# Three weight bits from ScalarE and the first block's low parts of g from VectorE, in a kernel of windowed attention and two MLPs

## The chip, the cores and the metric

The kernel runs on one core of one Trainium2 chip. The time is device microseconds of one execution; before the change the median of 3 runs is 924.38 us (921.47 to 929.18).

## The reference

Windowed attention (4 batches, 8 heads, 576 positions, head size 64, each position sees itself and the 63 before it) gives 2304 rows of 512 numbers. They go through two MLPs, and only the first of them and its weights are touched here:

```python
def _moe_ref(x, w_in, w_out) -> np.ndarray:          # x 2304 x 512
    h = x @ w_in                                       # 512 x 2048
    g = np.maximum(h, 0.0) + np.log1p(np.exp(-np.abs(h)))   # softplus
    return (g @ w_out).astype(np.float32)              # 2048 x 512
...
x = _moe_ref(x=x, **moe_kwargs)
return _moe2_ref(x=x, **moe2_kwargs)                 # sigmoid gate, 512 -> 1536 -> 512
```

The weights arrive as 8-byte floats, q, k and v as 4-byte ones.

## The kernel before, in words

**Products in three parts.** Every matrix product is made of rounded high parts and low parts: `mm3` (L362 to L365) runs high x high, high x low and low x high into the same PSUM bank. So each operand needs a high part (a rounding copy on ScalarE) and a low part (the value minus its high part).

**The first MLP.** Tokens go in five blocks of 512, 384, 384, 512 and 512 columns (b = 0 to 4). For each block and each of 16 slices f of 128 hidden units, `m1_proj` makes h (12 matmuls), `m1_act` (L382, ScalarE) the softplus into a tile "tb", `g_hi` (L389, ScalarE) its high part, `g_lo` (L395, GpSimd) its low part, and `m1_out` adds g x w_out into four PSUM banks (12 matmuls). Block b+1's attention runs between block b's products.

**The weights.** The 32 slices of w_in and w_out (i = 0 to 31, alternating after the first three; NSLOT is 32) are loaded once, during block 0, and then stay in SBUF. A slice is a 128x1024 tile of words, "raw", that holds low word and high word of each 8-byte float in turn. It is turned into 4-byte floats in "bits" by four steps and split by two more:

- `w_scale` (L118, ScalarE): the high word, read as a float and scaled by 2^-112, gives exponent and leading bits.
- `w_shift` (L123, VectorE): shifts these left by 3.
- `w_sign` (L127, VectorE): puts in the sign of the high word.
- `w_low` (L132, VectorE): puts in the low word's top three bits (shift right by 29, then or).
- `w_hi` (L138, ScalarE): the high part of the slice.
- `w_lo` (L143, GpSimd): its low part.

There are three raw tiles and three bits tiles; a raw tile is free after `w_low`, a bits tile after `w_lo`. The second MLP's 36 slices go through the same first four steps later.

**Attention, as far as it matters.** For a group of 64 positions TensorE makes scores into a PSUM tile "at" (two of them), VectorE's `att_max` (L272, L275) reads them, ScalarE takes the exponentials (L287), GpSimd's `att_norm` (L298) divides, TensorE turns the result round, and `att_values` (L345) writes into the next of the two "at" tiles. So `att_values` waits until `att_max` of an earlier group has read that tile. `att_hi` and `att_lo` (L353, L358) split the result.

**The order.** The program is one list of steps for all engines, and each engine runs its own in that order. For everything up to the second MLP the list comes from `lead_in`, a planner: it takes the steps with their costs and dependencies from `traits` (for example `"pool", 1.25` for g_lo) and plays them through, engine by engine, so that a change of costs or of engines moves steps of every engine. Filler matmuls on "ones" (L680) keep TensorE busy at the start.

## Time and profile before

| | us |
|---|---|
| median of 3 runs | 924.38 (921.47 to 929.18) |
| the profiled execution's own time | 923.64 |
| its span, first to last instruction | 921.9 |
| mean granted TensorE clock in the span | 0.993 of full speed |
| TensorE matmuls busy | 897.9 (97%) |
| VectorE, ScalarE, GpSimd busy | 507.7, 406.5, 358.9 |

The profile is of one execution, so its rows add up to its own time, 923.64 us, which stands 0.74 us below the median. Engines are PE (TensorE), PEld (its weight loads), DVE (VectorE), ACT (ScalarE), POOL (GpSimd) and SP (which issues DMAs). "x32 | 47.0, 1471 | 32.9 <-ACT" reads: 32 instructions, 47.0 us busy, 1471 ns mean, 32.9 us idle before them, ended mostly by ScalarE.

### The profile page before, as it was taken

What the parts mean: (1) busy time and instruction counts of PE and PEld (TensorE: products, weight loads), DVE (VectorE), ACT (ScalarE), POOL (GpSimd) and SP (SyncE); (2) the same over time, 40 slices, a digit from 0 to 9 for tenths busy, and PEclk for the clock granted to TensorE, in tenths of its full rate; (3) what the DMA queues carried; (4) which work ended last, traced back from release to release, by engine and by line L of the source; (5) the groups of instructions that cost most, each with busy time, mean ns of one, the idle gap of its engine ahead of it and who ended that gap; (6) DMA issues with size and microseconds to landing.
All of it is one profiled execution on the core that took longest, in us unless ns stands there. A gap on an engine that the chain in (4) does not pass through costs nothing.

```text
span 921.9 us, 13808 instructions
## 1 busy us (share of the span) xinstructions
PE 897.9 (97%) x5070; PEld 803.8 (87%) x5074; DVE 507.7 (55%) x843; ACT 406.5 (44%) x930; POOL 358.9 (39%) x312
## 2 busy tenths in 40 slices
PE   8998899999999999999999999999999999999998
PEld 6687678998989988888888999998999999999996
DVE  5999996335343645437801667656445446444443
ACT  6877666563855655634522333324222224222222
POOL 3576675342642544455831233325111115111111
PEclk9999999999999999999999999999999999999999
DMA  8645654566666676476403676545564445544441
GB/s 313 202 160 206 218 164 169 187 220 225 208 217 219 222 262 207 156 265 241 160 1 149 228 274 229 205 160 194 194 228 160 160 160 194 195 159 160 160 160 69
DMA packets 56643, 176.54 MB, mean 192 GB/s; under 512 B 6144, under 2 KB 21248, under 8 KB 51968
## 3 DMA queue, kind: packets, MB, share of 16 engines
q1 hardware_dynamic: 56576, 175.66, 54.7%
q8 instruction: 40, 0.66, 0.3%
q14 instruction: 27, 0.22, 0.1%
HBM read 138.67 MB, written 36.96 MB: 191 GB/s over the span
## 4 chain that ended last, share of the span: by engine, by line
PE 78%; DVE 8%; DMA 6%; ACT 5%; issue 3%; SPq 1%; POOL 0%; ACTq 0%; DVEq 0%
PE h L363 14%; PE h L364 14%; PE h L365 14%; PE acc L363 9%; PE acc L364 9%; PE acc L365 9%; DMA pd<-pd 3%; DVE bits L127 2%; DVE bits L123 2%; PE at L260 2%; PE at L365 2%; PE at L364 2%; PE at L363 2%; DVE bits L132 1%; ACT p L287 1%
## 5 line engine op out<-in xcount | busy, mean ns | idle before, releaser
L471 DVE TENSOR_TENSOR t<-h,t 128x384 f32<-128x384 f32 x216 | 116.9, 555 | 199.4 <-PE h L365 191.6
L477 POOL TENSOR_TENSOR g<-t,g 128x384 fp32r<-128x384 f32 x72 | 74.8, 1040 | 288.5 <-ACT g L476 278.3
L364 PE MATMUL h<-xc,wc 128*128 128x384 f32 x504 | 169.7, 337 | 0.0
L363 PE MATMUL h<-xc,wc 128*128 128x384 f32 x504 | 169.0, 335 | 0.5 <-DVE t L471 0.4
L365 PE MATMUL h<-xc,wc 128*128 128x384 f32 x504 | 169.3, 336 | 0.0
L395 POOL TENSOR_TENSOR g<-tb,g 128x512 fp32r<-128x512 f32 (+1 forms) x80 | 102.6, 1284 | 139.1 <-ACT g L389 104.6
L363 PE MATMUL acc<-g,w 128*128 128x512 f32 (+1 forms) x320 | 122.2, 382 | 0.0
L363 PE MATMUL h<-xt,w 128*128 128x512 f32 (+1 forms) x320 | 119.7, 374 | 0.8 <-DVE xt L358 0.6
L364 PE MATMUL acc<-g,w 128*128 128x512 f32 (+1 forms) x320 | 119.5, 373 | 0.0
L365 PE MATMUL acc<-g,w 128*128 128x512 f32 (+1 forms) x320 | 119.3, 373 | 0.0
L364 PE MATMUL h<-xt,w 128*128 128x512 f32 (+1 forms) x320 | 118.0, 369 | 0.0
L365 PE MATMUL h<-xt,w 128*128 128x512 f32 (+1 forms) x320 | 117.9, 369 | 0.0
L476 ACT CAST g<-t 128x384 fp32r<-128x384 f32 x72 | 37.0, 514 | 155.0 <-DVE t L471 138.0
L363 PEld LDWEIGHTS h<-xc,wc 128*128 128x128 f32 x504 | 94.6, 188 | 9.0 <-ACT t L483 1.0
L364 PEld LDWEIGHTS h<-xc,wc 128*128 128x128 f32 x504 | 94.5, 188 | 6.5
L365 PEld LDWEIGHTS h<-xc,wc 128*128 128x128 f32 x504 | 94.7, 188 | 0.0
L143 POOL TENSOR_TENSOR w<-bits,w 128x512 fp32r<-128x512 f32 x44 | 62.9, 1430 | 56.2 <-ACT w L138 44.7
L382 ACT ACTIVATE tb<-h 128x512 f32<-128x512 f32 (+1 forms) x80 | 44.1, 551 | 87.5 <-PE h L365 86.3
L132 DVE SCALAR_TENSOR_TENSOR bits<-raw,bits 128x512 uint32<-128x512 uint32 x68 | 69.5, 1022 | 1.8
L363 PEld LDWEIGHTS h<-xt,w 128*128 128x128 f32 x320 | 60.5, 189 | 9.3 <-DVE xt L358 1.1
L363 PEld LDWEIGHTS acc<-g,w 128*128 128x128 f32 x320 | 61.3, 191 | 8.2
L365 PEld LDWEIGHTS acc<-g,w 128*128 128x128 f32 x320 | 61.4, 192 | 7.8
(100 smaller groups left out, 1549.5 us busy)
## 6 DMA issues: line engine op xcount, KB each, us to landing
wc<-wcd SPq DMA_DIRECT2D x36, 1792.0 KB, 7.2
raw<-in_w SPq DMA_DIRECT2D x32, 512.0 KB, 3.7
qk<-in_qk SPq DMA_DIRECT2D x28, 512.0 KB, 5.0
wcd<-raw SPq DMA_DIRECT2D x24, 512.0 KB, 4.8
v<-in_vt SPq DMA_DIRECT2D x25, 256.0 KB, 4.2
raw<-in_wg SPq DMA_DIRECT2D x12, 512.0 KB, 4.4
raw<-in_wv SPq DMA_DIRECT2D x12, 512.0 KB, 4.6
wcd<-sumr SPq DMA_DIRECT2D x12, 512.0 KB, 5.2
```

The costliest lines, as they stand in the source:

```text
L123: nc.vector.tensor_scalar(out=t, in0=t, scalar1=3, scalar2=None, op0=ALU.logical_shift_left)
L127: nc.vector.scalar_tensor_tensor(out=t, in0=r[:, :, 1], scalar=0x80000000, in1=t, op0=ALU.bitwise_and, op1=ALU.bitwise_or)
L132: nc.vector.scalar_tensor_tensor(out=t, in0=r[:, :, 0], scalar=29, in1=t, op0=ALU.logical_shift_right, op1=ALU.bitwise_or)
L143: nc.gpsimd.tensor_tensor(out=w[:, 1, :], in0=t, in1=w[:, 0, :].bitcast(F32), op=ALU.subtract)
L363: nc.tensor.matmul(out=o, lhsT=lh, rhs=rh, start=first, stop=False)
L364: nc.tensor.matmul(out=o, lhsT=lh, rhs=rl, start=False, stop=False)
L365: nc.tensor.matmul(out=o, lhsT=ll, rhs=rh, start=False, stop=last)
L382: nc.scalar.activation(out=t, in_=h_t.pop((b, f)), func=AF.Softplus)
L395: nc.gpsimd.tensor_tensor(out=g[:, 1, :n], in0=t, in1=g[:, 0, :n].bitcast(F32), op=ALU.subtract)
L471: nc.vector.tensor_tensor(out=out, in0=a, in1=b, op=op)
L476: nc.scalar.copy(out=g[:, 0, :HALF], in_=t)
L477: nc.gpsimd.tensor_tensor(out=g[:, 1, :HALF], in0=t, in1=g[:, 0, :HALF].bitcast(F32), op=ALU.subtract)
```

## The change

Of the 32 slices of the first MLP every odd one (16) is "topped". ScalarE gets a new instruction for it, which reads the low words as integers, scales them by almost 2^-29 with a small offset, and writes them back as integers from 0 to 7: the three bits. VectorE's separate shift goes away for that slice; one instruction (`w_join`) shifts by 3 and puts the three bits in, and the sign follows. In block 0, `g_lo` goes from GpSimd to VectorE. The planner's costs follow. The second MLP's slices and blocks 1 to 4 keep the old steps.

```diff
+    def topped(i):
+        return i < NSLOT and i % 2
+
     def w_shift(i):
-        t = bits_t[i]
-        nc.vector.tensor_scalar(out=t, in0=t, scalar1=3, scalar2=None, op0=ALU.logical_shift_left)
+        t, r = bits_t[i], raw_t[i][:, :, 0]
+        if topped(i):
+            nc.scalar.activation(out=r, in_=r, func=AF.Copy, scale=2.0 ** -29 * (1 - 2.0 ** -7), bias=-0.4395)
+        else:
+            nc.vector.tensor_scalar(out=t, in0=t, scalar1=3, scalar2=None, op0=ALU.logical_shift_left)
+
+    def w_join(i):
+        t, r = bits_t[i], raw_t[i]
+        nc.vector.scalar_tensor_tensor(out=t, in0=t, scalar=3, in1=r[:, :, 0], op0=ALU.logical_shift_left,
+                                       op1=ALU.bitwise_or)
 
     def w_sign(i):
+        if topped(i):
+            w_join(i)
+        else:
+            put_sign(i)
+
+    def put_sign(i):
         t, r = bits_t[i], raw_t[i]
         nc.vector.scalar_tensor_tensor(out=t, in0=r[:, :, 1], scalar=0x80000000, in1=t, op0=ALU.bitwise_and,
                                        op1=ALU.bitwise_or)
 
     def w_low(i):
+        if topped(i):
+            put_sign(i)
+            del raw_t[i]
+            return
...
     def g_lo(b, f):
...
-        nc.gpsimd.tensor_tensor(out=g[:, 1, :n], in0=t, in1=g[:, 0, :n].bitcast(F32), op=ALU.subtract)
+        engine = nc.gpsimd if b else nc.vector
+        engine.tensor_tensor(out=g[:, 1, :n], in0=t, in1=g[:, 0, :n].bitcast(F32), op=ALU.subtract)
...
         if fn is w_shift:
-            return "dve", 0.5, 0, [(w_scale, a)], []
+            return "act" if topped(a) else "dve", 0.67 if topped(a) else 0.5, 0, [(w_scale, a)], []
...
         if fn is g_lo:
-            return "pool", 1.25, 0, [(g_hi, a, f)], []
+            return "pool" if a else "dve", 1.25 if a else 0.7, 0, [(g_hi, a, f)], []
```

In the changed file the lines are others: the shift is L132, the sign L147, the old last step L156, the join L136, ScalarE's new step L130, g_lo L420, w_hi L162, w_lo L167, the softplus L406, g_hi L413, `att_max` L296 and L299.

VectorE's order at slices 10, 11 and 12 (bits_751, bits_798, bits_808), before:

```order
L123 TENSOR_SCALAR bits_751<-bits_751 128x512
L127 SCALAR_TENSOR_TENSOR bits_751<-raw_689,bits_751 128x512
L132 SCALAR_TENSOR_TENSOR bits_751<-raw_689,bits_751 128x512
L272 SCALAR_TENSOR_TENSOR p_792<-at_771,mask_70 128x512
L275 TENSOR_REDUCE st_793<-p_792 128x4
L123 TENSOR_SCALAR bits_798<-bits_798 128x512
L127 SCALAR_TENSOR_TENSOR bits_798<-raw_705,bits_798 128x512
L132 SCALAR_TENSOR_TENSOR bits_798<-raw_705,bits_798 128x512
L123 TENSOR_SCALAR bits_808<-bits_808 128x512
L127 SCALAR_TENSOR_TENSOR bits_808<-raw_756,bits_808 128x512
L132 SCALAR_TENSOR_TENSOR bits_808<-raw_756,bits_808 128x512
```

The same slices now (bits_763, bits_805, bits_829):

```order
L132 TENSOR_SCALAR bits_763<-bits_763 128x512
L147 SCALAR_TENSOR_TENSOR bits_763<-raw_687,bits_763 128x512
L156 SCALAR_TENSOR_TENSOR bits_763<-raw_687,bits_763 128x512
L420 TENSOR_TENSOR g_771<-tb_769,g_771 128x512
L296 SCALAR_TENSOR_TENSOR p_801<-at_736,mask_70 128x512
L299 TENSOR_REDUCE st_802<-p_801 128x4
L136 SCALAR_TENSOR_TENSOR bits_805<-bits_805,raw_767 128x512
L147 SCALAR_TENSOR_TENSOR bits_805<-raw_767,bits_805 128x512
L132 TENSOR_SCALAR bits_829<-bits_829 128x512
L147 SCALAR_TENSOR_TENSOR bits_829<-raw_790,bits_829 128x512
L156 SCALAR_TENSOR_TENSOR bits_829<-raw_790,bits_829 128x512
L420 TENSOR_TENSOR g_832<-tb_826,g_832 128x512
```

Slice 11 has two instructions in place of three, and after each pair of slices stands one g_lo, which waits for ScalarE's g_hi and has the next slices behind it.

ScalarE's order at the same place, before (w9 to w11 are the high parts of slices 9 to 11):

```order
L118 ACTIVATE bits_751<-raw_689 128x512
L382 ACTIVATE tb_754<-h0_707 128x512
L138 CAST w9_759<-bits_726 128x512
L389 CAST g_763<-tb_754 128x512
L335 COPY pt_776<-at_765 128x512
L118 ACTIVATE bits_798<-raw_705 128x512
L138 CAST w10_801<-bits_751 128x512
L118 ACTIVATE bits_808<-raw_756 128x512
L382 ACTIVATE tb_816<-h1_779 128x512
L389 CAST g_831<-tb_816 128x512
L138 CAST w11_836<-bits_798 128x512
```

And now:

```order
L118 ACTIVATE bits_763<-raw_687 128x512
L406 ACTIVATE tb_769<-h0_701 128x512
L413 CAST g_771<-tb_769 128x512
L162 CAST w9_774<-bits_724 128x512
L359 COPY pt_792<-at_730 128x512
L162 CAST w10_799<-bits_763 128x512
L118 ACTIVATE bits_805<-raw_767 128x512
L130 ACTIVATE raw_767<-raw_767 128x512
L406 ACTIVATE tb_826<-h1_776 128x512
L118 ACTIVATE bits_829<-raw_790 128x512
L413 CAST g_832<-tb_826 128x512
```

The new instruction (L130) stands right behind slice 11's scaling. Slice 10's high part now stands ahead of slice 11's scaling, and g_hi ahead of slice 9's high part.

GpSimd's order there, before:

```order
L143 TENSOR_TENSOR w9_759<-bits_726,w9_759 128x512
L395 TENSOR_TENSOR g_763<-tb_754,g_763 128x512
L143 TENSOR_TENSOR w10_801<-bits_751,w10_801 128x512
L395 TENSOR_TENSOR g_831<-tb_816,g_831 128x512
L143 TENSOR_TENSOR w11_836<-bits_798,w11_836 128x512
L143 TENSOR_TENSOR w12_861<-bits_808,w12_861 128x512
```

And now:

```order
L167 TENSOR_TENSOR w9_774<-bits_724,w9_774 128x512
L167 TENSOR_TENSOR w10_799<-bits_763,w10_799 128x512
L167 TENSOR_TENSOR w11_853<-bits_805,w11_853 128x512
L167 TENSOR_TENSOR w12_863<-bits_829,w12_863 128x512
L167 TENSOR_TENSOR w13_903<-bits_834,w13_903 128x512
```

The low parts of g are gone from between the weights' low parts; only attention's divisions remain there.

## Rows read from the trace of the kernel before

**Rows 1.** The page: each engine's busy time, share of the span, instructions.

```profile
PE 897.9 (97%) x5070; PEld 803.8 (87%) x5074; DVE 507.7 (55%) x843; ACT 406.5 (44%) x930; POOL 358.9 (39%) x312
```

**Rows 2.** Windows: length; PE, PEld, DVE, ACT, POOL busy; clock; DMA share; GB/s.

```profile
25.00:145.00 120.00, 109.47 (x656) 87.79 (x657) 112.11 (x141) 85.90 (x184) 81.30 (x57) 0.97 0.58 192
...
105.00:110.00 5.00, 2.79 (x20) 2.39 (x21) 4.93 (x7) 4.16 (x7) 3.78 (x3) 0.70 0.91 289
...
140.00:145.00 5.00, 4.92 (x19) 4.09 (x20) 4.90 (x9) 3.54 (x6) 3.01 (x3) 0.66 0.33 113
```

**Rows 3.** Waits of TensorE between 25 and 145 us: total, times, longest.

```profile
PE at L345 <- DVE p L272: 6.2, 2, 3.5
PE at L260 <- DVE xt L358: 2.9, 1, 2.9
```

**Rows 4.** Waits of TensorE after 145 us, the longest.

```profile
PE at L345 <- DMA pt<-pd: 5.2, 3, 2.0
```

**Rows 5.** Instructions of TensorE in time: start, length, line; idle before, releaser.

```profile
77.47 0.68 PE L345 MATMUL at<-pt,v 64*64 64x64 f32 x16 [2.70 <-DVE p L272]
...
78.42 0.40 PE L364 MATMUL h<-xt,w 128*128 128x512 f32 x1
...
79.35 0.39 PE L365 MATMUL h<-xt,w 128*128 128x512 f32 x1
...
108.26 0.80 PE L363 MATMUL h<-xt,w 128*128 128x512 f32 x1
...
110.48 0.40 PE L365 MATMUL h<-xt,w 128*128 128x512 f32 x1
...
141.00 0.70 PE L363 MATMUL acc<-g,w 128*128 128x512 f32 x1
...
144.73 0.40 PE L363 MATMUL acc<-g,w 128*128 128x512 f32 x1
...
145.42 0.34 PE L363 MATMUL h<-xt,w 128*128 128x384 f32 x1
```

**Rows 6.** VectorE's three groups on bits between 25 and 145 us.

```profile
L132 DVE SCALAR_TENSOR_TENSOR bits<-raw,bits 128x512 uint32<-128x512 uint32 x32 | 39.3, 1229 | 0.9
L127 DVE SCALAR_TENSOR_TENSOR bits<-raw,bits 128x512 uint32<-128x512 uint32 x32 | 34.2, 1070 | 1.1
L123 DVE TENSOR_SCALAR bits<-bits 128x512 uint32<-128x512 uint32 x33 | 26.1, 790 | 3.7 <-ACT bits L118 3.7
```

**Rows 7.** Instructions of VectorE in time.

```profile
40.49 0.41 DVE L123 TENSOR_SCALAR bits<-bits 128x512 uint32<-128x512 uint32 x1
...
41.66 0.69 DVE L132 SCALAR_TENSOR_TENSOR bits<-raw,bits 128x512 uint32<-128x512 uint32 x1
42.27 0.68 DVE L272 SCALAR_TENSOR_TENSOR p<-at,mask 128x512 f32<-128x512 f32 x1
...
99.40 1.65 DVE L132 SCALAR_TENSOR_TENSOR bits<-raw,bits 128x512 uint32<-128x512 uint32 x1
```

**Rows 8.** Instructions of GpSimd in time.

```profile
41.81 1.70 POOL L395 TENSOR_TENSOR g<-tb,g 128x512 fp32r<-128x512 f32 x1 [1.80 <-ACT g L389]
...
99.03 1.47 POOL L143 TENSOR_TENSOR w<-bits,w 128x512 fp32r<-128x512 f32 x1 [1.28 <-ACT w L138]
```

**Rows 9.** GpSimd's two largest groups between 25 and 145 us.

```profile
L143 POOL TENSOR_TENSOR w<-bits,w 128x512 fp32r<-128x512 f32 x32 | 47.0, 1471 | 32.9 <-ACT w L138 25.7 <-PE acc L365 7.3
L395 POOL TENSOR_TENSOR g<-tb,g 128x512 fp32r<-128x512 f32 x16 | 25.5, 1593 | 4.6 <-POOL p L298 2.1 <-ACT g L389 1.8 <-POOL w L143 0.3
```

**Rows 10.** ScalarE's groups between 25 and 145 us.

```profile
L118 ACT ACTIVATE bits<-raw 128x512 f32<-128x512 f32 x33 | 22.0, 670 | 4.6 <-POOL w L143 1.9 <-DMA raw<-in_w 1.5 <-POOL g L395 1.1
L138 ACT CAST w<-bits 128x512 fp32r<-128x512 f32 x32 | 19.8, 617 | 24.8 <-DVE bits L132 24.8
L389 ACT CAST g<-tb 128x512 fp32r<-128x512 f32 x16 | 9.9, 618 | 0.3
L382 ACT ACTIVATE tb<-h 128x512 f32<-128x512 f32 x16 | 9.4, 590 | 1.0 <-PE h L365 0.8
```

## The prediction

> **What bounds the kernel now.** I read the page first: TensorE is busy for 97% of the span, VectorE for 55% [rows 1]. By that alone nothing on VectorE could matter. But these are averages, and the change touches one stage, block 0, in which the 32 weight slices are made. So I read that stage in windows. Between 25 and 145 us VectorE is busy for 112.1 of 120 us, TensorE for 109.5, ScalarE for 85.9, GpSimd for 81.3 [rows 2]. Here VectorE is the fuller engine. Next the waits: in this stretch TensorE stands at `att_values` for 6.2 us in two pieces (of 3.5 and 2.7), because `att_max` on VectorE hasn't yet read the "at" tile, and once for 2.9 us on `att_lo` [rows 3]. Both steps are short; they are late because weights are queued ahead of them. That is 9.1 us in which TensorE is idle through VectorE. After two of these gaps the matmuls start slowly [rows 5]: five take 2.22 us after the second gap, of 3.5 (108.26 to 110.48), and nine take 3.73 us after the third, of 2.9 (141.00 to 144.73). After the first gap, of 2.7, four take 0.93 us (78.42 to 79.35), 0.23 each, which is full speed. The granted clock of those five-us windows is 0.70 and 0.66, so part of them ran at the lower level of 1.2 GHz behind a pause [rows 2]. The slow starts cost 2.22 - 5 x 0.23 = 1.07 and 3.73 - 9 x 0.23 = 1.66, together 2.7 us. So 9.1 + 2.7 = 11.8 us is the most that a faster VectorE can give in this stage. After 145 us the largest wait of TensorE is on attention's DMAs, 5.2 us [rows 4], which the change doesn't address.
>
> **Why VectorE is full.** The same instruction takes two very different times. Undisturbed, the shift takes 0.41 us and the two others 0.69 [rows 7]; in the stage their means are 0.79, 1.07 and 1.23 [rows 6]. The L132 that starts at 99.40 and takes 1.65 us [rows 7] meets a GpSimd instruction that had begun at 99.03 and takes 1.47 [rows 8]. The L272 at 42.27 runs beside a GpSimd instruction of 41.81 to 43.51 [rows 8] and takes its ordinary 0.68 [rows 7]: its input is in PSUM. So what is stretched are VectorE's instructions with SBUF operands, by instructions of GpSimd. How much in all: 99.6 us are spent in the three groups (39.3 + 34.2 + 26.1), and undisturbed they would take 33 x 0.41 + 64 x 0.69 = 57.7 us. The excess of 41.9 us, over the 57 instructions of GpSimd in the stretch [rows 2], is 0.74 us for each.
>
> The Trainium skill says ("SBUF — State Buffer", § Who interferes with whom) that a VectorE instruction with two SBUF inputs and a GpSimd instruction that reads SBUF take a shared port as an exclusive lock, each for its whole length. The trace agrees that the one stops the other, and that a PSUM input is spared; as to size it shows 0.74 us for each, not the whole 1.47 to 1.59 of a GpSimd instruction. By whole lengths the sixteen that go would give back 16 x 1.59 = 25 us, and the sum below would come out at the ceiling.
>
> **The change, part by part.**
>
> *Sixteen shifts leave VectorE.* That is 16 x 0.41 = 6.6 us of undisturbed time. The join that replaces the old last step is an instruction of the same kind, with the same strided words, at 0.69; so a topped slice costs 2 x 0.69 in place of 0.41 + 2 x 0.69.
>
> *Sixteen g_lo leave GpSimd.* 25.5 us of its time go [rows 9], and with them 16 occasions to stretch VectorE: 16 x 0.74 = 11.8 us.
>
> *Sixteen g_lo come to VectorE.* The trace has no such instruction there at 128x512 with both inputs in SBUF; the nearest rows are L127 and L132, same shape, two SBUF inputs: 0.69 undisturbed, 1.65 when caught [rows 7]. I take 0.69, because being caught is already counted once for each GpSimd instruction that remains: 16 x 0.69 = 11.0 us. If every one were caught beyond that it would be 26.4.
>
> Sum for VectorE in the stage: -6.6 - 11.8 + 11.0 = -7.4 us. The bounds: if the 41 GpSimd instructions that remain each catch VectorE for the full 1.65 - 0.69 = 0.96 us, the excess is 39.4 in place of 41.9, and the sum is -2.5 - 6.6 + 11.0 = +1.9. If each catches it for a half less than now (0.37), the excess is 15.2, and the sum far below what TensorE can use, so -11.8 is the end there.
>
> *What TensorE makes of it.* 7.4 us of the 9.1 us of gaps go, if they shrink by what VectorE gains ahead of each. What remains is 1.7 us over three places, each shorter than the first gap, which had no slow start, so the 2.7 us of them go too. -7.4 - 2.7 = -10.1 us.
>
> *Sixteen instructions come to ScalarE.* Same engine, shape and stride as `w_scale`, which takes 0.67 [rows 10]: 16 x 0.67 = 10.7 us, so ScalarE would be busy for 96.6 us of about 110, 88%. What hides them: ScalarE waits 24.8 us for VectorE's last bits step ahead of `w_hi` [rows 10]. Bounds: 0.59, the softplus's mean [rows 10], to twice 0.67 if writing every other word costs as much again; I take 0.67. The order shows that the instruction stands right behind its slice's `w_scale` or one or two steps later; ahead of the softplus of the next f in the piece shown. One that stands there delays h's chain by 0.67 us, but g has three buffers and `m1_out` runs two slices behind `m1_proj`, 24 matmuls or 5.5 us at 0.23 each, so that is covered.
>
> *g_lo as a new wait on VectorE.* Behind each g_lo stand the next two slices; whatever g_lo waits for, they wait too. It needs softplus and g_hi, 0.59 + 0.62 us after the projection ends [rows 10]. The planner puts g_lo one to two slices after the projection, so mostly it is ready; behind a block of exponentials the softplus comes late, and I follow one such place (f = 3, behind the first exponentials) in the order: VectorE would stand there for about 0.7 us. I count that once as TensorE's time: +0.7.
>
> *What else moves.* The weight loads on SP, and the scores of the second attention group, which TensorE now does ahead of the first projection and not after the third: a move of work, no more of it. Raw tiles are still freed by a slice's last VectorE step and bits tiles by `w_lo`, so the three buffers of each turn no slower. After the first slices of block 1 the order of every engine is as before; there TensorE is busy with 349 of 355 us, and I cost it at nothing.
>
> The sum against the profiled execution's own time: 923.64 - 10.1 + 0.7 = 914.2; with the 0.74 us by which the median lies higher, 915.0.
>
> **The rivals.**
>
> *All of TensorE's lost time goes.* VectorE gains more than the mean says, since a GpSimd with fewer instructions also runs its own faster (1.59 and 1.47 now, stretched by VectorE in turn). Then 11.8 us: 924.4 - 11.8 = 912.6. Against it: three attention blocks, with their runs of exponentials on ScalarE, still starve VectorE of slices (its waits for L118, 3.7 us [rows 6]).
>
> *ScalarE holds the slices back.* 88% in an engine that takes its steps in order is little slack; each new step stands ahead of some slice's `w_hi` or `w_scale`. If half of the 10.7 us comes out on VectorE's path, the gain falls to 9.4 - 5.4 = 4.0: 920.4. For it: VectorE already waits for L118. Against: 24.8 us of ScalarE's own waits are for VectorE.
> The Trainium skill ("ScalarE: Activation LUTs", § Rules for kernel authors) says that adding and multiplying belong on VectorE and not on ScalarE. Undisturbed the rows agree, 0.41 against 0.67; the mean in the stage, 0.79, is the other way. By the rule the move loses 16 x 0.26 = 4.2 us of engine time, which is this rival.
>
> *VectorE stands at every g_lo (the slower end).* If TensorE is what VectorE waits for, a loop closes: projection, softplus, g_hi, g_lo, then the slices that the next projections need. Each turn that VectorE comes before g_hi is done costs up to 0.59 + 0.62 + about 0.1 for signals = 1.3 us. At all sixteen: +20.8, against -7.4: 924.4 + 13.4 = 937.8. It decides from 7.4 / 16 = 0.46 us of waiting per g_lo on. Against it: GpSimd's g_lo waited only 1.8 us in all for g_hi [rows 9].
>
> *The gain is eaten later.* If attention's transfers after 145 us keep their time of day, TensorE waits longer there; up to all of it, 924. DMA share is 0.58 in the stage [rows 2], so nothing is full; I give this little.
>
> **How the numbers follow.** The forecast's own family (913.5 to 918) has 0.46, TensorE's whole loss gone 0.20, ScalarE 0.20, g_lo's waits 0.09, eaten later 0.05. A change of 1%, 9.2 us, is about what a measurement of this kernel can tell from none; it lies at 915.1, just above the forecast, so of the 0.46 I put 0.25 on faster and 0.21 on no difference. Faster: 0.25 + 0.20 = 0.45; same: 0.21 + 0.20 + 0.05 = 0.46; slower: 0.09. The range runs from 911.0, a little under the ceiling's 912.6, to 923.0, above ScalarE's 920.4; outside are g_lo's waits and the ends of the others.
>
> **What would show it.** Right: TensorE's first matmul of block 1 (128x384), at 145.42 now [rows 5], comes near 136; the waits of TensorE on VectorE's `att_max` and `att_lo` before it fall under 2 us; the sign and last steps (L147, L156) have means well under 1.07 and 1.23; the new L130 is 16 x 0.67; g_lo on VectorE is near 0.7 to 1.0; no window at 0.7 clock in the stage. Wrong: the means on VectorE stay where they are (then the stretch isn't per GpSimd instruction); VectorE's idle time at L420 is over 7 us; ScalarE has no waits for VectorE left and VectorE's waits for L118 or L130 grow past 8 us; or the first block-1 matmul comes early and the end doesn't.

## The result and the profile after

The changed kernel takes 917.08 us (median of 20 runs, 914.0 to 921.92) beside 925.39 us for the kernel before on the same chip (20 runs, 921.47 to 930.89). The ratio is 0.9917, with a 95% interval from 0.9898 to 0.9936. The gain is 0.8%, 8.3 us between the medians; the forecast was 915.0 us, 1.0%. The profiled execution of the changed kernel took 919.43 us (span 917.7, mean granted clock 0.992), 4.2 us less than the profiled one of before (923.64).

The page's first part, to be read against [rows 1]: averages that tell as little as before. VectorE has given up 13 us, GpSimd 26, and ScalarE has taken 8.

```profile
PE 900.3 (98%) x5076; PEld 804.7 (88%) x5076; DVE 494.8 (54%) x843; ACT 414.4 (45%) x946; POOL 333.2 (36%) x296
```

The windows, with the columns of [rows 2], for the start and for the stretch from 25 to 145 us:

```profile
5.00:10.00 5.00, 3.67 (x25) 3.49 (x24) 2.22 (x4) 2.58 (x14) 0.00 (x0) 0.90 0.98 325
10.00:15.00 5.00, 5.00 (x25) 5.00 (x25) 2.66 (x6) 1.93 (x11) 0.61 (x1) 0.50 1.06 361
15.00:20.00 5.00, 5.00 (x25) 3.85 (x25) 2.24 (x7) 2.27 (x11) 1.88 (x2) 0.58 1.04 398
25.00:145.00 120.00, 117.82 (x740) 93.74 (x738) 102.17 (x152) 101.41 (x233) 56.19 (x42) 1.00 0.56 192
```

Over the 120 us VectorE falls from 112.1 to 102.2, GpSimd from 81.3 to 56.2, ScalarE rises from 85.9 to 101.4, TensorE from 109.5 to 117.8, and the clock in the stage is 1.00. The first three rows show something else: at the start TensorE ran near its lower level of 1.2 GHz for ten microseconds (0.50 and 0.58). That comes back below.

TensorE's waits between 25 and 150 us, to be read against [rows 3]:

```profile
PE at L369 <- DVE p L296: 1.5, 2, 0.8
PE h L389 <- POOL w L167: 0.6, 1, 0.6
PE h L387 <- ACT tb L406: 0.4, 1, 0.4
```

The two waits for `att_max`, 6.2 us, are now 1.5 us; the 2.9 us at `att_lo` are gone; a wait of 0.6 us for a weight's low part is new.

TensorE in time, as in [rows 5] (the last two rows are later, in block 1 and block 2):

```profile
41.63 0.58 PE L387 MATMUL h<-xt,w 128*128 128x512 f32 x1
...
81.94 0.68 PE L369 MATMUL at<-pt,v 64*64 64x64 f32 x16 [0.79 <-DVE p L296]
...
93.45 0.50 PE L389 MATMUL h<-xt,w 128*128 128x512 f32 x1 [0.58 <-POOL w L167]
...
109.85 0.69 PE L369 MATMUL at<-pt,v 128*64 128x64 f32 x16 [0.70 <-DVE p L296]
...
140.23 0.33 PE L387 MATMUL h<-xt,w 128*128 128x384 f32 x1
...
229.24 0.44 PE L387 MATMUL h<-xt,w 128*128 128x384 f32 x1 [2.36 <-ACT tb L406]
...
281.91 1.04 PE L369 MATMUL at<-pt,v 128*64 128x64 f32 x16 [2.48 <-DMA pt<-pd]
```

I call "the stage" what lies between the first matmul of the first projection and the first matmul of 384 columns. Before it ran from 37.25 to 145.42, 108.17 us; now it runs from 41.63 to 140.23, 98.60 us. So the stage gives 9.6 us, and the start takes 4.4 of them away in this execution.

The groups of VectorE, ScalarE and GpSimd between 25 and 145 us, as in [rows 6, 9, 10]:

```profile
L147 DVE SCALAR_TENSOR_TENSOR bits<-raw,bits 128x512 uint32<-128x512 uint32 x33 | 33.7, 1020 | 1.1
L156 DVE SCALAR_TENSOR_TENSOR bits<-raw,bits 128x512 uint32<-128x512 uint32 x17 | 17.6, 1034 | 0.6
L136 DVE SCALAR_TENSOR_TENSOR bits<-bits,raw 128x512 uint32<-128x512 uint32 x16 | 14.4, 903 | 1.8 <-issue 1.8
L420 DVE TENSOR_TENSOR g<-tb,g 128x512 fp32r<-128x512 f32 x15 | 12.4, 830 | 4.4 <-ACT g L413 4.4
L132 DVE TENSOR_SCALAR bits<-bits 128x512 uint32<-128x512 uint32 x17 | 7.8, 456 | 0.2
...
L162 ACT CAST w<-bits 128x512 fp32r<-128x512 f32 x32 | 19.7, 616 | 15.4 <-DVE bits L156 9.2 <-DVE bits L147 6.1
...
L130 ACT ACTIVATE raw<-raw 128x512 uint32<-128x512 uint32 x16 | 10.8, 676 | 0.0
...
L167 POOL TENSOR_TENSOR w<-bits,w 128x512 fp32r<-128x512 f32 x32 | 45.6, 1425 | 52.2 <-ACT w L162 52.2
```

The five groups of VectorE take 85.9 us. Undisturbed, by the forecast's 0.69 and 0.41, they would take 81 x 0.69 + 17 x 0.41 = 62.9. The excess is 23.0 us, over 42 instructions of GpSimd 0.55 us for each; before it was 41.9 us over 57, or 0.74. GpSimd's own low parts became a little shorter too, 1425 ns after 1471.

These figures for each are means over instructions that were caught and others that were not. One by one it looks sharper. Here a low part on GpSimd and a weight's last step on VectorE meet:

```profile
44.12 1.48 POOL L167 TENSOR_TENSOR w<-bits,w 128x512 fp32r<-128x512 f32 x1 [1.28 <-ACT w L162]
44.49 1.67 DVE L156 SCALAR_TENSOR_TENSOR bits<-raw,bits 128x512 uint32<-128x512 uint32 x1
```

GpSimd ends at 45.60, VectorE at 46.16. In the example of [rows 7, 8] the ends are 100.50 and 101.05. So it is with every VectorE instruction with two SBUF inputs that takes over 0.9 us in the stage, 30 of 59 before and 23 of 73 now: each began beside a reading instruction of GpSimd that was already under way, and ends 0.55 us after that one's end. Of the shifts 15 of 30 were caught before and end 0.28 to 0.29 us behind it; now none is. An instruction that is caught stands until GpSimd is done. What the change lowered is the number caught: 45 before, 23 now.

### The profile page after: what moved, and what is told of

Its sections match the earlier page's. It is cut to its first block, busy times and chain, and to the rows that moved or that the text cites. A ratio compares the mean times of both kernels' runs of the same rounds, so it can differ in the third digit from the quotient of the medians.

```text
span 917.7 us, 13810 instructions
## 1 busy us (share of the span) xinstructions
PE 900.3 (98%) x5076; PEld 804.7 (88%) x5076; DVE 494.8 (54%) x843; ACT 414.4 (45%) x946; POOL 333.2 (36%) x296
## 4 chain that ended last, share of the span: by engine, by line
PE 72%; DMA 10%; DVE 8%; ACT 6%; issue 3%; SPq 1%; POOL 0%; DVEq 0%; ACTq 0%; POOLq 0%
PE h L387 13%; PE h L388 13%; PE h L389 13%; PE acc L387 8%; PE acc L388 8%; PE acc L389 8%; DMA pd<-pd 4%; DMA wcd<-raw 2%; DVE bits L147 2%; PE at L389 2%; PE at L388 2%; ACT p L311 2%; PE at L387 2%; PE at L284 1%; PE acc L284 1%
## 5 line engine op out<-in xcount | busy, mean ns | idle before, releaser
L420 POOL TENSOR_TENSOR g<-tb,g 128x384 fp32r<-128x384 f32 (+1 forms) x64 | 77.8, 1218 | 134.0 <-ACT g L413 98.7
L167 POOL TENSOR_TENSOR w<-bits,w 128x512 fp32r<-128x512 f32 x44 | 61.4, 1396 | 75.5 <-ACT w L162 71.2
L406 ACT ACTIVATE tb<-h 128x512 f32<-128x512 f32 (+1 forms) x80 | 44.1, 551 | 90.3 <-PE h L389 90.1
L387 PEld LDWEIGHTS h<-xt,w 128*128 128x128 f32 x320 | 60.1, 188 | 11.0 <-ACT tb L406 3.5
L389 PEld LDWEIGHTS h<-xt,w 128*128 128x128 f32 x320 | 60.1, 188 | 9.2 <-POOL w L167 1.7
```

Source lines behind the costliest of these rows:

```text
L167: nc.gpsimd.tensor_tensor(out=w[:, 1, :], in0=t, in1=w[:, 0, :].bitcast(F32), op=ALU.subtract)
L387: nc.tensor.matmul(out=o, lhsT=lh, rhs=rh, start=first, stop=False)
L389: nc.tensor.matmul(out=o, lhsT=ll, rhs=rh, start=False, stop=last)
L406: nc.scalar.activation(out=t, in_=h_t.pop((b, f)), func=AF.Softplus)
L420: engine.tensor_tensor(out=g[:, 1, :n], in0=t, in1=g[:, 0, :n].bitcast(F32), op=ALU.subtract)
```

## The experiments

All times are medians, with the ratio to the kernel before on the same chip. The stage is read from one profiled execution of each kernel. "TensorE idle" is the sum of its gaps over 0.3 us inside the stage; "slow clock" is, summed over the five-us windows of the stage below 0.97, (1 - granted clock) x 5 us, which is too much where part of a window was idle.

| kernel | ratio (95%) | stage, us | TensorE idle | slow clock | rest |
|---|---|---|---|---|---|
| before | | 108.17 | 9.0 | 3.4 | 95.8 |
| the change | 0.9917 (0.9898 to 0.9936) | 98.60 | 2.1 | 0 | 96.5 |
| e1 topping alone | 1.0024 (0.999 to 1.0058) | 109.60 | 9.7 | 1.7 | 98.2 |
| e2 g_lo alone | 0.9977 (0.9945 to 1.0009) | 107.12 | 9.0 | 1.6 | 96.5 |
| e3 order alone | 1.0017 (0.9986 to 1.0048) | 107.91 | 7.5 | 5.0 | 95.4 |
| e4 change again | 0.9891 (0.9842 to 0.994) | 98.74 | 2.2 | 0 | 96.5 |
| e5 topping, change's order | 1.0027 (1.0003 to 1.0052) | 108.02 | 9.0 | 1.7 | 97.3 |
| e6 g_lo, change's order | 0.9985 (0.995 to 1.0021) | 102.43 | 4.7 | 1.7 | 96.0 |
| e7 change + 16 reads | 1.0045 (1.0005 to 1.0084) | 107.04 | 7.1 | 3.4 | 96.5 |
| e8 change + 32 writes | 0.9905 (0.9877 to 0.9932) | 98.80 | 2.5 | 0 | 96.3 |
| e9 change + 8 reads | 0.9958 (0.9932 to 0.9983) | 102.33 | 4.0 | 1.7 | 96.7 |
| e10 ScalarE twice | 0.9951 (0.9923 to 0.9979) | 102.90 | 5.0 | 1.7 | 96.2 |
| e11 all 32 topped | 0.9916 (0.9892 to 0.9939) | 102.33 | 3.9 | 0 | 98.4 |
| e12 start filled | 0.9893 (0.987 to 0.9916) | 98.59 | 2.1 | 0 | 96.5 |

The last column is the stage less the two before it. It lies between 95.4 and 98.4 in all of them: what a kernel changes in this stage is TensorE's idle time and the slow clock, with differences of up to 3 us besides.

**Each part alone, in the order that the planner makes for it.** Two lines undo g_lo's move (e1), one undoes the topping (e2):

```diff
-        engine = nc.gpsimd if b else nc.vector
+        engine = nc.gpsimd
...
-            return "pool" if a else "dve", 1.25 if a else 0.7, 0, [(g_hi, a, f)], []
+            return "pool", 1.25, 0, [(g_hi, a, f)], []
```

```diff
-        return i < NSLOT and i % 2
+        return False
```

Of e1 (topping alone):

> The change with g_lo of block 0 left on GpSimd: the sixteen topped slices alone. My theory (VectorE's load in block 0 is what TensorE waits for; sixteen shifts are 6.6 us of it, and GpSimd's stretching stays as it was): about 6.6 us less of TensorE's waits, and the slow starts behind them partly gone, so 6 to 9 us under before. Rival A (what counts is the stretching of VectorE by GpSimd, and that stays): at most 3 us under before. Rival B (ScalarE holds the slices back): no gain or slower.

Measured: 928.34 us, ratio 1.0024. Of e2 (g_lo alone):

> The change without any topped slice: g_lo of block 0 on VectorE alone. My theory: -11.8 us of stretching and +11.0 us of new work on VectorE, so within 2 us of before. Rival A (the stretching counts most, since VectorE and GpSimd block each other): 5 us or more under before. Rival C (VectorE stands at every g_lo): 5 us or more above before.

Measured: 925.22 us, ratio 0.9977. The 6 to 9 us expected of the topping did not come. Neither part alone brings a gain that the runs can tell from none, and both together bring 8 to 10 us. But the planner puts the steps in another order each time, so this mixes the parts with the order.

**The order alone, and the change a second time.** e3 keeps the instructions of before and gives the planner the changed costs and engines, so that only the order is the change's:

```diff
         if fn is w_shift:
-            return "dve", 0.5, 0, [(w_scale, a)], []
+            t = a < NSLOT and a % 2
+            return "act" if t else "dve", 0.67 if t else 0.5, 0, [(w_scale, a)], []
...
-            return "pool", 1.25, 0, [(g_hi, a, f)], []
+            return "pool" if a else "dve", 1.25 if a else 0.7, 0, [(g_hi, a, f)], []
```

> The instructions of before, on the engines of before, in the order that the planner makes for the change. My theory: no load is taken from VectorE, so within 3 us of before, and rather slower, since the order was made for other engines. Rival D (the new order, with attention's scores and turns earlier, is what brings the gain): 5 us or more under before.

Measured: 927.17 us, ratio 1.0017, stage 107.91. The order alone gives nothing while the instructions are those of before. e4 is the changed kernel once more:

> The changed kernel once more, for its start. In the first trace of it the granted clock was 0.50 to 0.58 between 10 and 20 us and the first projection began at 41.6 us, against 37.3 before, though the first 35 us hold the same instructions. If that is chance, this trace shows the first projection near 37 us, or the same late start with a time of 3 to 5 us more than the fastest runs; if the change causes it, the late start is there again in the profile and all runs.

Measured: 915.68 us (913.29 to 919.12). Its profiled execution started at full clock; the first projection begins at 36.93 us and the first matmul of 384 columns stands here:

```profile
135.67 0.33 PE L387 MATMUL h<-xt,w 128*128 128x384 f32 x1
...
225.24 0.69 PE L387 MATMUL h<-xt,w 128*128 128x384 f32 x1 [2.41 <-ACT tb L406]
```

That is "near 136", as forecast, and the stage of 98.74 us repeats the 98.60. The second row is a later loss, told below.

**Each part alone in the change's order.** e5 sets `engine = nc.gpsimd` in `g_lo` and leaves the planner's table as the change has it; e6 does the same for the topping (`if topped(i):` becomes `if False:` in the three steps).

> The changed kernel in its own order, with only block 0's g_lo put back on GpSimd. The stage from the first projection to the first matmul of 384 columns took 108.2 us before, 98.6 and 98.7 in the two traces of the change, 109.6 with topped slices alone in the planner's own order for them. New theory (two things in series hold TensorE: VectorE's load, and the way of a slice's low part through GpSimd's queue, where it stands behind g_lo): the stage is 104 us or more, with TensorE waiting for GpSimd's low parts of w. Rival (topped slices alone were only ordered badly by the planner): the stage is under 101 us.

Measured: 924.82 us, ratio 1.0027, stage 108.02.

> The changed kernel in its own order, with only the topped slices undone (VectorE makes all the shifts, g_lo of block 0 stays on it). New theory: VectorE's load is back at 112 us between 25 and 145 us and is what TensorE waits for; the stage is 105 to 109 us, with waits of TensorE for VectorE and none for GpSimd. Rival (g_lo off GpSimd is the gain, and the planner's order for it alone was poor): under 101 us.

Measured: 921.62 us, ratio 0.9985, stage 102.43: neither the 105 to 109 us of the expectation nor its rival's less than 101. The same instructions in the planner's own order for them (e2) have a stage of 107.12, so the order is worth 4.7 us there. With e3 and the change these are four kernels in one order: neither 107.9, topping 108.0, g_lo 102.4, both 98.6. So the topping is worth nothing while GpSimd still does g_lo, and 3.8 us once it does not. In e5 VectorE is no longer the fuller engine, yet TensorE waits as long as before (a window of 25 to 145 us; waits from 25 to 152 us):

```profile
25.00:145.00 120.00, 110.75 (x699) 86.65 (x698) 96.74 (x128) 94.16 (x212) 78.17 (x55) 0.99 0.53 182
```

```profile
PE h L389 <- POOL w L167: 5.3, 4, 2.7
PE at L369 <- DVE p L296: 3.4, 2, 1.7
PE acc L389 <- POOL w L167: 0.4, 1, 0.4
```

VectorE is busy for 96.7 of 120 us, and in the stage itself for 88.1 of 108.0, after 102.3 of 108.2 before. What is late now is mostly the weights' low part on GpSimd, 5.7 of 9.0 us, with g_lo in the same queue. But VectorE too stands now, at the join, for ScalarE's new instruction, which it does not do in the change:

```profile
L136 DVE SCALAR_TENSOR_TENSOR bits<-bits,raw 128x512 uint32<-128x512 uint32 x15 | 14.5, 970 | 8.0 <-ACT raw L130 8.0
```

The wait moved; it did not go. How much of it goes back to GpSimd's queue and how much to ScalarE, no run here separates.

**GpSimd's reads against GpSimd's time.** Does g_lo's leaving help because GpSimd gets free, or because it reads SBUF less beside VectorE? e7 gives GpSimd sixteen useless subtractions behind the g_lo of block 0, on a tile of its own; e8 gives it two memsets there instead, which only write:

```diff
+        if b == 0:
+            nc.gpsimd.tensor_tensor(out=spare, in0=spare, in1=spare, op=ALU.subtract)
```

```diff
+        if b == 0:
+            for _ in range(2):
+                nc.gpsimd.memset(spare, 0.0)
```

> The changed kernel with 16 more instructions on GpSimd where g_lo stood in its order, of the same kind and shape (a subtraction of 128x512, both inputs in SBUF), whose result nobody needs. They bring back both the stretching of VectorE and the delay in GpSimd's queue, but no wait for softplus or g_hi. Both parts of the new theory: the stage is 102 to 107 us and VectorE's means of sign and last step rise from 1.02 and 1.03 by 0.1 or more. If GpSimd matters only through g_lo's own waits: under 100 us.

Measured: 926.82 us, ratio 1.0045, stage 107.04.

> As with the extra reads, but each of the 16 is two memsets of the same tile, which write SBUF and read nothing. If what costs is the shared reading of SBUF (the stretching), VectorE's means stay near 1.02 and 1.03 and the stage under 101 us; if what costs is the time in GpSimd's queue, the stage is as long as with the extra reads, as far as two memsets take as long as one subtraction.

Measured: 915.2 us, ratio 0.9905, stage 98.80. GpSimd's and VectorE's groups of e7 between 25 and 145 us, and TensorE's largest wait between 25 and 152 us:

```profile
L148 DVE SCALAR_TENSOR_TENSOR bits<-raw,bits 128x512 uint32<-128x512 uint32 x31 | 33.4, 1078 | 1.0
L157 DVE SCALAR_TENSOR_TENSOR bits<-raw,bits 128x512 uint32<-128x512 uint32 x15 | 19.0, 1268 | 0.5
L421 DVE TENSOR_TENSOR g<-tb,g 128x512 fp32r<-128x512 f32 x15 | 17.0, 1136 | 4.4 <-ACT g L414 4.4
...
L423 POOL TENSOR_TENSOR spare<-spare 128x512 f32<-128x512 f32 x15 | 21.4, 1429 | 0.0
```

```profile
PE at L370 <- DVE p L297: 6.0, 2, 3.0
```

The same groups of e8:

```profile
L148 DVE SCALAR_TENSOR_TENSOR bits<-raw,bits 128x512 uint32<-128x512 uint32 x33 | 34.6, 1050 | 1.1
L157 DVE SCALAR_TENSOR_TENSOR bits<-raw,bits 128x512 uint32<-128x512 uint32 x17 | 18.6, 1097 | 0.6
L421 DVE TENSOR_TENSOR g<-tb,g 128x512 fp32r<-128x512 f32 x15 | 12.3, 822 | 4.6 <-ACT g L414 4.5
...
L424 POOL MEMSET spare<- 128x512 f32 x30 | 15.8, 525 | 0.9
```

The reads bring the 6 us at `att_max` back, and with the slow clock behind them (3.4 us) nearly the whole stage. The memsets, 15.8 us of GpSimd's time, leave VectorE's excess over undisturbed, worked out as above over all five groups, at 23.0 us, the very number of the change; in e7 it is 33.4. In e8's stage 15 of VectorE's instructions with two SBUF inputs ran beside a memset and still took about 0.69 us. The memsets are somewhat less time than the 21.4 us of reads, and they come in shorter pieces. Against GpSimd's time as the cause speaks also the next run: its eight reads are 10.6 us of GpSimd's time, less than the memsets, and cost the stage 3.7 us where the memsets cost 0.2.

**Half of the reads** (`if b == 0 and f % 2:`):

> The change, and behind every second g_lo of block 0 one 128x512 subtraction on GpSimd on a tile of its own (8 in place of the 16 of e7_pool_extra_reads; they add work and change no output). The stage (first projection's first matmul to the first matmul of 384 columns) took 98.6 and 98.7 us for the change and 107.0 with sixteen. If every reading instruction of GpSimd costs the stage the same, the 8.3 us are divided by sixteen and eight cost 4.2: stage 102.9, ratio about 0.995. If what decides is a threshold (VectorE has slack until a certain number of them), eight cost 0 to 1.5 us, the stage takes 98.7 to 100.2 and the ratio is about 0.991. I expect something between, nearer the even share: 101 to 103.

Measured: 920.8 us, ratio 0.9958, stage 102.33. Eight reads cost the stage 3.6 to 3.7 us, sixteen 8.3 to 8.4: 0.46 and 0.53 us for each. That is near an even share, and shows no threshold; each number rests on one profile.

**How much slack has ScalarE?** e10 copies each topped slice's bits once more onto themselves; e11 tops all 32 slices:

```diff
             nc.scalar.activation(out=r, in_=r, func=AF.Copy, scale=2.0 ** -29 * (1 - 2.0 ** -7), bias=-0.4395)
+            nc.scalar.activation(out=r, in_=r, func=AF.Copy, scale=1.0)
```

```diff
-        return i < NSLOT and i % 2
+        return i < NSLOT
```

> The change, and each of the sixteen three-bit instructions on ScalarE is followed by a second one that copies its result onto itself (integers stay as they are, so no output changes): 16 x 0.67 = 10.7 us more of ScalarE's time in the stage, ahead of the joins. Theory that ScalarE has slack: it is busy for 101.4 of 120 us now and would be for 112; the stage stays under 100.5 us. Rival, ScalarE holds the slices back (the forecast's second rival): the gain falls by half of the added time or more, stage 104 or longer, VectorE's waits for L130 and ScalarE's other lines grow past 8 us. I think the rival is the likelier one here, since little slack is left: stage 101 to 106.

Measured: 919.49 us, ratio 0.9951, stage 102.90. TensorE's waits in e10 between 25 and 150 us:

```profile
PE at L370 <- DVE p L297: 2.8, 2, 1.4
PE at L370 <- ACT pt L360: 1.5, 1, 1.5
PE h L390 <- POOL w L168: 0.7, 1, 0.7
```

> The change with all 32 slices topped by ScalarE, not 16 (in the planner's order for that). VectorE loses another 16 x 0.46 = 7.3 us, ScalarE gets another 16 x 0.676 = 10.8 on top of 101.4 of 120. If VectorE's time is what still counts in the stage, it falls by up to the 2.1 us that TensorE still waits in it, to 96.6. If ScalarE's slack is used up at sixteen, the stage gets longer: 101 to 106. If neither is on the path, 98.7 as now. I expect 99 to 103 and a ratio of 0.990 to 0.997.

Measured: 916.74 us, ratio 0.9916, stage 102.33. Another 10.9 us on ScalarE cost the stage 4.2 us in e10, partly in a wait for ScalarE itself (1.5 us at the turned-round result); VectorE stands 2.6 us at the join for the added instructions. So sixteen new instructions fit, and thirty-two of them do not fit for nothing. In e11, where VectorE gets something for them, the time of the kernel stays that of the change. Its stage is 3.7 us longer: 1.8 us are idle time (3.3 of its 3.9 us are waits for the weights' low parts), and 1.9 us lie beside idle time and clock; where those come from was not followed up.

**The start.** e12 puts fillers ahead of the first attention groups' scores too:

```diff
-                elif key[0] in (att_transpose, att_values, m1_proj) and key[1] < NG0 and start < START:
+                elif key[0] in (att_scores, att_transpose, att_values, m1_proj) and key[1] < NG0 and start < START:
```

> The change, and filler matmuls on ones also ahead of the first attention groups' scores, where TensorE now waits for transfers or stands (62 fillers there in place of 52; they add work and change no output). In the profile of the change the granted clock fell to 0.50 in the window from 10 to 15 us, behind a wait of 1.32 us for a transfer, and the first projection began at 41.63 us; in another profile of the same kernel it began at 36.93. If the idle time at the start brings the lower clock, the fillers keep it away: first projection at 36.5 to 37.5 and no run with a late start, so a median 1 to 2.5 us under the change's, ratio 0.987 to 0.990. If it comes whatever TensorE does there, the ratio is 0.990 to 0.994, and the fillers cost up to 2 us where they stand in front of work.

Measured: 914.48 us, its four runs between 914.1 and 915.29, ratio 0.9893. Its windows at the start, to be read against the change's above:

```profile
5.00:10.00 5.00, 4.95 (x39) 4.50 (x39) 2.22 (x4) 2.39 (x13) 0.00 (x0) 1.00 0.97 312
10.00:15.00 5.00, 4.95 (x39) 4.12 (x40) 4.15 (x10) 3.93 (x20) 1.65 (x2) 1.00 1.07 334
15.00:20.00 5.00, 5.00 (x55) 4.66 (x54) 3.47 (x9) 2.76 (x11) 2.08 (x2) 1.00 1.04 395
```

The clock stays at 2.4 GHz (eight matmuls of 128x128 take 1.05 us at 10.42), the first projection begins at 37.23 us and the first matmul of 384 columns at 135.82. Of the change's 24 runs (20 and the 4 of e4) only four lie at or under 915.29. This agrees with fillers keeping the clock, but four runs that did not stand beside the change's on one chip, and one profile, do not show it: e4 began at 36.93 us without them. Its interval reaches over the change's, so it isn't shown to be faster.

The late start is no rarity, and it isn't the change's alone: of the fourteen profiles five begin the first projection after 40 us (the change, e2, e3, e5 and e8), the other nine between 36.4 and 37.3. Nor do the windows always show it. In e8, which began at 42.43, they say 1.00 from 5 to 20 us, but its matmuls last as long as those that the change did at 0.50, and twice as long as e4's. Eight matmuls of 128x128 in the change, in e8 and in e4:

```profile
11.88 2.02 PE L284 MATMUL acc<-qk 128*128 128x128 f32 x8
...
12.30 2.02 PE L285 MATMUL acc<-qk 128*128 128x128 f32 x8
...
10.61 1.11 PE L284 MATMUL acc<-qk 128*128 128x128 f32 x8
```

In e2 and e5 it is the same (2.02 us each, at a granted clock of 1.00 by the windows). At the start the matmuls' own lengths are the surer sign.

## Why the prediction was right, and where its working was not

The time, 917.08 us, lies in the range and 2.1 us above the forecast, and most of its own signs came: the first matmul of 384 columns "near 136" (135.67 in e4, 135.82 in e12; 140.23 in the change's profile, which had started 4.4 us late), TensorE's waits for `att_max` and `att_lo` under 2 us (1.5), L130 at 16 x 0.67 (0.676), g_lo on VectorE at 0.7 to 1.0 (0.83), no slow window in the stage. One hardly did: the sign's mean was to be well under 1.07 us and is 1.02. Point by point:

**What bounds the stage, and the ceiling of 11.8 us: shown.** Before, 108.17 - 9.1 - 2.7 gives 96.4 us without lost time (95.8 by the table's coarser count); in the change and in seven other kernels what is left without idle time and slow clock is 96.2 to 96.7, in the other five 95.4 to 98.4. The stage gained 9.6 us where the forecast said 9.4. Of that 7.0 are idle time (9.1 to 2.1) and 2.7 the slow starts, beside the forecast's 7.4 less 0.7, and 2.7.

**The sum for VectorE, "-6.6 - 11.8 + 11.0 = -7.4": the step that failed.** It has two faults. That TensorE's time came out right all the same was in part luck: VectorE gained twice the sum, and TensorE had only 9.1 us of gaps to give back.
- The term "16 x 0.74 = 11.8" was mis-sized. The excess fell by 41.9 - 23.0 = 18.9 us. I left each remaining GpSimd instruction its 0.74; it went down to 0.55. The price isn't one for each GpSimd instruction at all, but about 0.9 us for each VectorE instruction that is caught (1.58 and 1.61 us in place of 0.69 for those with two SBUF inputs), and 22 fewer were caught, not 16. In the stage VectorE's busy time fell from 102.3 to 86.3 us, 16 us and not 7.4. This is what the first rival said of VectorE ("VectorE gains more than the mean says"); its price, 11.8 us, came but for the 2.1 us of gaps that are left.
- The sum adds the parts up as if each were worth its own term: the topping 6.6, g_lo's move 0.8. The four kernels in one order show the topping worth 0 alone (108.0 beside 107.9), g_lo's move 5.5 alone, and the topping 3.8 on top of it. With g_lo left on GpSimd (e5) VectorE is busy 14 us less than before, and TensorE waits 9.0 us all the same, 5.7 of them for the weights' low parts, while VectorE stands 8.0 us for ScalarE's new instruction. As I read it, a full VectorE was the cause only together with the others: GpSimd and VectorE hold each other up, and a weight needs ScalarE, VectorE and GpSimd, one after the other. That is argued from the waits; no run takes ScalarE's share out.

**That the stretch comes from GpSimd's instructions: shown, and narrowed.** Of the stage's gain of 9.6 us sixteen added reading instructions take back 8.4, eight 3.7, and 30 memsets 0.2. The Trainium skill says ("SBUF — State Buffer", § Who interferes with whom) that a VectorE instruction with two SBUF inputs contends with a GpSimd instruction that reads SBUF and not with one that only writes it. e7 and e8 agree with both halves. The forecast cited the exclusive lock from there and set it aside as to size, because the mean was 0.74 us and not a whole instruction. That reading was wrong: a mean over all of GpSimd's instructions, of which many catch nothing, says nothing on the lock. Where one is caught the trace agrees with a lock: 53 of 53 instructions of VectorE, in the two stages, end 0.55 us behind GpSimd's.

**ScalarE hides sixteen instructions: right, with little to spare.** L136, which needs L130's result, stands 1.8 us in the whole stretch, and no part of it is put down to L130 (in e5, with less on VectorE, it is 8.0 us); ScalarE still waits 15.3 us for VectorE ahead of L162, after 24.8 [rows 10]. The second rival (920.4 us) is what e10 does when ScalarE gets sixteen more: 919.49.

**g_lo as a new wait: seen, and without the price.** VectorE stands 4.4 us at L420 for g_hi inside the stage, in three waits of up to 2.9 us, in the change as in e4 and e12; a fourth, of 2.7 us, comes after the stage's end in all three and makes it 7.1. So it does not stand at all sixteen; the third rival is out. With the fourth that is just over the 7 us which I had named as a sign against me, and it cost TensorE little: its remaining wait on VectorE is 1.5 us.

**After 145 us, "I cost it at nothing": wrong by 1 to 5 us.** In every kernel with the change's order (the change, e3 to e10 and e12) TensorE stands 2.0 to 2.4 us at the softplus's tile in block 1, which before it did not. ScalarE of the change in time, there:

```profile
221.28 0.67 ACT L118 ACTIVATE bits<-raw 128x512 f32<-128x512 f32 x1 [5.40 <-DMA raw<-in_wv]
221.85 0.48 ACT L406 ACTIVATE tb<-h 128x384 f32<-128x384 f32 x1
...
227.40 1.28 ACT L406 ACT_TABLE_LOAD   x1
228.69 0.49 ACT L406 ACTIVATE tb<-h 128x384 f32<-128x384 f32 x1
```

The softplus stands behind a slice of the second MLP whose load landed late, then the exponentials, the table load and the next softplus, for which TensorE waits at 229.24. In the kernel before the same row stands 4.8 us for its load (at 227.14), and TensorE is not held there; it had lost as much a little earlier, at a transfer of attention:

```profile
216.11 1.09 PE L345 MATMUL at<-pt,v 128*64 128x64 f32 x16 [2.03 <-DMA pt<-pd]
```

That wait is gone (change) or 0.4 us (e4). So, as I read it, one loss took the place of another; no run tests it. The next two waits for such transfers, 2.0 and 1.1 us before [rows 4], are 1.6 and 2.5 now, and 1.2 and 3.6 in e4. Together TensorE's gaps from the stage's end to block 3 are 5.2 us before, 6.9 in the change's profile, 8.0 in e4's. With the slow matmuls behind such gaps and what is later still, the whole stretch from the stage's end to the last instruction takes 776.5 us before, 777.5 in the change's profile, 777.7 in e12's and 781.6 in e4's. This is the fourth rival in small: 1.0 to 5.1 us of the 9.6 are lost again. e4 lost here what it had won at the start; e12, which began as early, did not, so an early start isn't what decides it. e3, the order without the gain in the stage, is at 1.0017, which is on that side, though its interval takes in 1.

**The start: not in the forecast at all.** The change's profile lost 4.4 us before the stage, e4's and e12's nothing. Five of the fourteen profiles lose 3 to 6 us there; which share of the change's own executions does is open. It and the later waits are enough for the 2.1 us between 917.1 and 915.0; how they divide in the runs without a profile can't be read.

## What to carry to other kernels

Where two engines read SBUF side by side and stretch each other, count the reading instructions that go from the one, not its busy time: here each was worth about 0.5 us of the stage, and writes cost nothing that could be seen. Look at single instructions before taking a mean for a price: a caught instruction may stand for nearly the whole of the other one, and what a change lowers is the number caught. Don't add up the parts of a change along a chain in which a product needs several engines one after the other: one part alone only shows which engine is late next. When one half of a change is undone, keep the other half's order of steps: g_lo alone had a stage of 107.1 us in its own order and 102.4 in the change's. And a gain of some us in one stage comes out at the end only as far as the loads and the engine orders behind it are early as well; look for a step that waits for a transfer with work queued behind it.

## What was not expected of the hardware

- A VectorE instruction with two SBUF inputs that GpSimd's reads catch ends 0.55 us after the GpSimd instruction's end, in all 53 cases of the two stages, whether that one still had 0.4 us to go or 1.2.
- GpSimd's memset of 128x512 (525 ns, thirty of them) did not stretch VectorE's two-input instructions at all (excess 23.0 us with and without); a subtraction of the same shape did.
- ScalarE's in-place copy of every other word as integers takes 676 ns, the float scaling of the same shape 670: no price for the conversion or for the stride of the output.
- VectorE's shift, which has one SBUF input, was stretched too: 790 ns in the stage before [rows 6] and 737 in e5, where GpSimd has g_lo; 456 in the change and 598 in e6, where it has not; 0.41 us undisturbed. In e7, with sixteen other reads, it is 488, so the number of reads alone does not set it.
- With the same instructions in the same order at the start, one execution of the change had granted clocks of 0.90, 0.50 and 0.58 in the windows from 5 to 20 us, behind one wait of 1.32 us for a transfer at 8.7 us; e4's waited there twice, 0.22 and 0.72 us, and had 1.00 in all three. It costs 4.4 to 4.7 us. e5 and e8 began 5.2 and 5.5 us later than e4 with 1.00 in all three, and with matmuls of double length.
- In the stage a slow window followed pauses of 1.5 (e9) and 1.4 us (e10), and none followed one of 1.72 in e5 or 2.7 in the kernel before [rows 5]. The pause's length alone does not tell.
